# One-engine tasks per 128 tokens of a batch, emitted in the order of a list scheduler, for a gated linear attention followed by a SiLU MLP

## The chip, the core and the metric

The kernel runs on one core of a Trainium2 chip. The metric is device time in microseconds of one execution. Three runs of the kernel before gave 249.70, 249.94 and 250.22 us; their median is 249.94 us.

## The reference

Two parts follow one another. The first is a recurrent attention over 768 time steps, for 4 batches and 8 heads of dimension 48, with a state of 48x48 for each batch and head. The second is an MLP on the 3072 tokens that come out, each with 8 x 48 = 384 numbers:

```python
f = 1.0 / (1.0 + np.exp(-f_logit))
for t in range(S):
    state = f[:, :, t, :, None] * state + np.einsum('bhd,bhe->bhde', k[:, :, t], v[:, :, t])
    y[:, :, t] = np.einsum('bhd,bhde->bhe', q[:, :, t], state)
x = y.transpose(0, 2, 1, 3).reshape(B * S, H * D)      # 3072 x 384
h = x @ w_in                                           # 384 x 2048
out = (h * (1.0 / (1.0 + np.exp(-h)))) @ w_out         # 2048 x 384
```

Inputs and output are fp32. The four attention inputs have 4.7 MB each, each weight matrix 3.1 MB.

## The kernel before

Time is cut into 6 chunks of 128 steps. A **unit** below is one chunk of one batch, so 128 tokens; there are 24 units. In the kernel before, four units (the four batches of a chunk `g`) go through most steps together.

For a chunk, `load` (L85, on SyncE's queue) brings `f`, `k`, `q` and `v` as one transfer each of 768 KB. `logs` (L142, L143, ScalarE) makes log(1+exp(-f)), the negative logarithm of the gate, with one Exp and one Ln. For each unit `decay` multiplies it with a triangle of ones on TensorE (`cs`, L149, a running sum over time), takes Exp of it with both signs (`ia` L151, `a` L154, ScalarE), and scales k (`ki`, L152, GpSimd) and q (`qg`, L155, VectorE). `values` casts v (L158, GpSimd) into a padded tile `vp`, `lasts` (L164, L167) gets the decay over the whole chunk, `al`. `transposes` (L179, L181) turns q and k, `scores` (L189, L193) makes the 128x128 scores of each head and masks them, `outputs` (L209, L212) sums the state's part and the scores' part straight into the transposed `y_ps`, of which VectorE makes `xT`, the operand of the MLP. `state` (L220 to L227) brings the state on by a chunk.

The MLP works on the 512 tokens of a chunk. `mlp_in` has 16 tiles `h_ps` of three 512-column matmuls (L258) each, and a Silu on ScalarE for each (L261). `mlp_out` has 16 matmuls of 384 columns (L268) for each unit, a copy (L273) and a store on SyncE's queue (L275). The weights come by GpSimd's queue, cast to bf16 on the way (`load_w_in` L119, `load_w_out` L124).

The order of each engine's instructions is the order in which the Python code issues them. `interleave_gen` mixes generators by the cost that each yields: the MLP of chunk `g` is mixed with the attention of chunk `g + 1` and the preparation of chunk `g + 2`:

```python
first = [(mlp_in(g), MLP)]
...
    first.append((part(att, ac / 2), ac / 2))
...
second = [(mlp_out(g), MLP)]
...
    second.append((prep(g + 2, wait), prep_cost(wait)))
```

All of chunk 0's attention, the weights' issue and chunk 1's preparation are written ahead of the first `mlp_in`. ScalarE needs another function table for Exp, for Ln and for Silu as the compiled program has it; each `ACT_TABLE_LOAD` stands ahead of the instruction that needs it and carries its line.

## Time and profile before

| what | value |
|---|---|
| median of three runs | 249.94 us (249.70 to 250.22) |
| span of the profiled execution | 247.9 us; the median of the runs is 2.0 us above it |
| TensorE matmul busy | 194.1 us (78%), 1616 instructions |
| VectorE busy | 111.8 us (45%), 193 instructions |
| ScalarE busy | 126.7 us (51%), 189 instructions, 23 of them table loads |
| GpSimd busy | 56.5 us (23%), 67 instructions |
| mean granted TensorE clock | 0.986 |
| HBM traffic | 25.17 MB read, 4.72 MB written |

The span runs from the first instruction to the last; a run's time also holds what lies around it. The profiled execution's own time is not given apart from its span, so the 2.0 us between span and median stand for what lies around. Busy shares are means over stages that differ: TensorE is nearly idle in the first quarter and nearly full in the rest. A matmul's recorded length includes its way through the array, so the speed of a row of matmuls is read from the distance of their starts.

### The profile page before, as it was taken

The page shows a single profiled execution, that of the slowest core. Times are in us where ns is not written, and L with a number is a line of the kernel's source. Part 1 is how long each engine was busy: PE and PEld are TensorE (multiplying, and loading weights), DVE is VectorE, ACT ScalarE, POOL GpSimd, SP SyncE. Part 2 cuts the span into 40 slices and gives each one's busy share as a digit, 9 for nine tenths or more (in the row PEclk, how much of TensorE's full clock was granted, in tenths as well). Part 3 has the DMA queues.
Part 4 walks back from the last instruction along what each step waited for, and adds up shares of the span by engine and source line. Part 5 has one row for each costly group of instructions (what it writes and reads, how often), then busy time and mean ns, then how long its engine had stood idle before and what let it go on. Part 6 is the DMA issues. An engine that isn't in the chain of part 4 may idle for free.

```text
span 247.9 us, 3938 instructions
## 1 busy us (share of the span) xinstructions
PE 194.1 (78%) x1616; PEld 116.6 (47%) x1632; DVE 111.8 (45%) x193; ACT 126.7 (51%) x189; POOL 56.5 (23%) x67
## 2 busy tenths in 40 slices
PE   0045452008999948898999989999989999999994
PEld 0034341005546725455665546755656555663462
DVE  5064752106545434444855449563476453520011
ACT  4963147015659078766376663776543454007600
POOL 1050999046000063002700018100072000000000
PEclk9999999999999985999999999999999999999999
DMA  9999999999990104995119991189601000110011
GB/s 144 187 186 187 188 197 186 184 201 187 190 130 34 49 15 97 189 176 79 36 66 172 187 180 35 66 145 187 85 32 67 32 3 0 61 38 32 0 63 63
DMA packets 105906, 26.99 MB, mean 109 GB/s; under 512 B 99232, under 2 KB 105888, under 8 KB 105888
## 3 DMA queue, kind: packets, MB, share of 16 engines
q1 hardware_dynamic: 102208, 23.60, 61.4%
q0 software_dynamic: 3680, 3.15, 7.8%
q8 instruction: 12, 0.20, 0.4%
q14 instruction: 6, 0.05, 0.1%
HBM read 25.17 MB, written 4.72 MB: 121 GB/s over the span
## 4 chain that ended last, share of the span: by engine, by line
PE 67%; DMA 11%; SPq 10%; ACT 8%; issue 1%; DVE 1%; POOL 0%; ACTq 0%; POOLq 0%
PE h_ps L258 26%; PE o_ps L268 23%; DMA v_ld<-in_v_dram 11%; SPq L85 10%; PE y_ps L209 7%; PE t_ps L179 4%; PE a_ps L189 3%; ACT L151 2%; ACT ia L151 2%; PE cs L149 2%; ACT a L154 1%; PE d_ps L223 1%; PE d_ps L220 1%; PE al_ps L164 1%; ACT lf L143 1%
## 5 line engine op out<-in xcount | busy, mean ns | idle before, releaser
L261 ACT ACTIVATE hT<-h_ps 128x512 bf16<-128x512 f32 x96 | 57.2, 597 | 45.9 <-PE h_ps L258 43.8
L258 PE MATMUL h_ps<-xT,w_in_sb 128*128 128x512 bf16 x272 | 73.9, 388 | 2.6 <-ACT hT L261 1.2
L268 PE MATMUL o_ps<-w_out_sb,hT 128*128 128x384 bf16 x384 | 71.7, 328 | 0.0
L268 PEld LDWEIGHTS <-hT 128*128 128x128 bf16 x384 | 35.7, 98 | 26.8 <-issue 5.7
L155 DVE TENSOR_TENSOR qg<-q_ld,a 128x384 bf16<-128x384 f32 x24 | 21.7, 905 | 41.4 <-ACT a L154 41.4
L149 PE MATMUL cs<-lf,triu 128*128 128x384 bf16 x24 | 9.2, 385 | 39.8 <-ACT a L154 28.2
L258 PEld LDWEIGHTS <-w_in_sb 128*128 128x128 bf16 x288 | 26.2, 100 | 29.5 <-issue 8.0
L193 DVE TENSOR_TENSOR atm<-a_ps,triu 128x512 bf16<-128x512 f32 x48 | 30.9, 686 | 19.8 <-PE a_ps L189 19.6
L152 POOL TENSOR_TENSOR ki<-k_ld,ia 128x384 bf16<-128x384 f32 x24 | 25.3, 1054 | 50.9 <-ACT ia L151 50.9
L158 POOL CAST vp<-v_ld 128x384 bf16<-128x384 f32 x24 | 16.0, 670 | 80.0 <-DMA v_ld<-in_v_dram 63.2
L273 DVE COPY o_sb<-o_ps 128x384 f32<-128x384 f32 x24 | 13.3, 555 | 29.7 <-PE o_ps L268 29.4
L151 ACT ACTIVATE ia<-cs 128x384 f32<-128x384 f32 x24 | 11.8, 490 | 27.4 <-PE cs L149 11.4
L209 PE MATMUL y_ps<-atm,vp 128*128 128x128 bf16 x240 | 23.9, 234 | 0.2
L181 DVE COPY qk<-t_ps 128x1024 bf16<-128x1024 bf16 x24 | 16.5, 688 | 13.7 <-PE t_ps L179 13.7
L227 DVE TENSOR_TENSOR st<-d_ps,al 48x192 bf16<-48x192 f32 x40 | 14.1, 352 | 14.6 <-PE d_ps L223 14.2
L212 DVE CAST xT<-y_ps 128x384 bf16<-128x384 f32 x24 | 13.2, 552 | 12.5 <-PE y_ps L209 12.5
L209 PEld LDWEIGHTS <-vp 128*128 128x128 bf16 x240 | 17.8, 105 | 0.9 <-issue 0.9
L179 PEld LDWEIGHTS <-qg 128*128 128x128 bf16 x96 | 8.2, 108 | 19.5 <-DVE qg L155 12.0
L151 ACT ACT_TABLE_LOAD x7 | 9.0, 1283 | 15.7 <-PE cs L149 15.7
L209 PE MATMUL y_ps<-qk,st 128*128 128x128 bf16 x120 | 16.5, 219 | 0.0
L223 PEld LDWEIGHTS <-ki 128*128 128x128 bf16 x80 | 6.2, 107 | 21.6 <-issue 19.4
L179 PE MATMUL t_ps<-ident,qg 128*128 128x128 bf16 x96 | 10.7, 242 | 3.6 <-DVE qk L181 2.1
(35 smaller groups left out, 142.1 us busy)
## 6 DMA issues: line engine op xcount, KB each, us to landing
out_dram<-o_sb SPq DMA_DIRECT2D x24, 192.0 KB, 1.9
f_ld<-in_f_logit_dram SPq DMA_DIRECT2D x5, 768.0 KB, 10.8
k_ld<-in_k_dram SPq DMA_DIRECT2D x5, 768.0 KB, 6.4
q_ld<-in_q_dram SPq DMA_DIRECT2D x5, 768.0 KB, 10.8
v_ld<-in_v_dram SPq DMA_DIRECT2D x5, 768.0 KB, 11.0
w_in_sb<-in_moe_w_in_dram POOLq DMA_DIRECT2D x4, 384.0 KB, 9.5
w_out_sb<-in_moe_w_out_dram POOLq DMA_DIRECT2D x2, 768.0 KB, 17.7
f_ld<-in_f_logit_dram SPq DMA_DIRECT2D x2, 384.0 KB, 5.3
```

Of the source, the lines that this page charges most:

```text
L85: nc.sync.dma_start(out=t[:, b0:b1].rearrange("p b h d -> p (b h) d"), in_=src)
L151: nc.scalar.activation(ia, cs, AF.Exp, scale=1.0)
L152: nc.gpsimd.tensor_mul(ki[i][:, b, :, 0:D], loaded[g, "k"][:, b], ia)
L155: nc.vector.tensor_mul(qg[i][:, b, :, 0:D], loaded[g, "q"][:, b], a)
L158: nc.gpsimd.tensor_copy(v_data(g % 2, b), loaded[g, "v"][:, b])
L179: nc.tensor.transpose(t_ps[:, j, p, :], src[i][:, b, 2 * p:2 * p + 2, :], ident)
L181: nc.vector.tensor_copy(sb, t_ps)
L193: nc.vector.tensor_mul(sb[:, r], a_ps[:, r], triu[:, None, :].to_broadcast([C, NP, C]))
L209: nc.tensor.matmul(y_ps[:, t, :], l, r, start=(n == 0), stop=(n == len(terms) - 1))
L258: nc.tensor.matmul(h_ps, w_in_sb[:, kk, n * 128:(n + 1) * 128], xT[g][:, kk].rearrange("p b c -> p (b c)"), start=(kk == 0), stop=(kk == K ...
L261: nc.scalar.activation(hT[g][:, n, :], h_ps, AF.Silu)
L268: nc.tensor.matmul(o_ps, hT[g][:, n, b * C:(b + 1) * C], w_out_sb[:, n, :], start=(n == 0), stop=(n == NT - 1))
```

## The change

The kernel is rewritten. Each step of each unit becomes a **task** of one engine with a duration, a priority, the tasks it waits for and the buffer slots it takes. `schedule` plays these tasks through in Python when the kernel is built: at each moment it gives a free engine the ready task of lowest priority number; for ScalarE it stays with one kind of function (Exp and Ln together, or Silu) by a few rules of its own, and counts 1.29 for each change of kind. `planned` sorts the tasks by the start that comes out, and they are emitted in that order.

The mathematics of a unit changes in these places. The output `y` is made token-major: four 96-column matmuls with the state and eight 48-column ones with the scores (`y`), copied to bf16 (`yc`), transposed by three matmuls (`yT`) and copied into `xT` (`xc`). The decay `a` is written by ScalarE over `cs` in PSUM, and VectorE reads it there for `qg`. The chunk's last decay is four one-column matmuls into the same bank and an `al` for each unit. The state is a VectorE addition (`sd`, instead of the matmul with `ident`, L220) and two multiplications on GpSimd (`su`). The MLP works on **pairs** of units, 256 tokens: a tile `mlp` holds two tiles of the hidden layer, six 256-column matmuls (`mi`) and one Silu of 512 columns (`si`). Three PSUM banks serve `mlp`, for the MLP's input and output. Loads are one transfer for each unit and tensor for units 0 to 3, then for each pair. The weights are eight transfers issued on GpSimd after `ki` of unit 2 or 4. Stores move to GpSimd's queue, but for the last two. With `turned=24` no unit takes the branch that transposes by DMA.

```diff
-def interleave_gen(*streams):
...
+CFG = dict(
+    margin=0.35,
+    pace=4.43,
+    turned=24,
+    dma_rate=187.0,
+    w_after=(2, 2, 2, 2, 2, 2, 2, 4),
...
+    rank=dict(ld=-19.78, E=-11.45, cs=-8.27, ia=-3.88, ki=-66.76, vb=-27.12, qg=6.22, tq=-14.46, qkc=71.64,
...
+SLOTS = dict(f=6, k=6, q=6, v=6, e=2, lf=3, ia=2, qk=5, vb=6, qkT=4, atm=3, yb=3, xT=4, hT=4, sd=2, al=6, o=4,
+             st0=1, st1=1, st2=1, st3=1, mlp=3, sc=1, tq=1, cs=1, yd=1)
...
+TABLE = 1.29
+class Task:
+    def __init__(self, name, eng, dur, prio, deps=(), acq=(), use=(), mode=None, phase=None, load=0.0):
...
+        groups = [(u0,), (u0 + 1,)] if P < 2 else [(u0, u0 + 1)]
+        for us in groups:
+            for n, x in enumerate("fkqv"):
+                add((x, us), "SP", 0.35 * len(us), base(us[0]) + R['ld'] + n * 0.1, acq=[I[x, P]], load=kb(192 * len(us)))
...
+        ia = add(("ia", u), "ACT", 0.387, B + R["ia"], deps=[cs], acq=[I["ia", u]], use=[I["cs", u]], mode="exp", phase=ph)
...
+    for n in range(4):
+        add(("wi", n), "POOL", 0.8, R["wi"] + n, deps=[T["ki", cfg["w_after"][n]]], load=786.432e3 / 341e3)
...
+                if t.mode is not None and t.mode != st["mode"]:
+                    st["mode"] = t.mode
+                    begin += TABLE
...
+def planned(cfg, slots):
+
+    tasks, T = make_tasks(cfg)
+    schedule(tasks, slots, cfg, cfg["margin"])
+    return sorted(tasks, key=lambda t: (t.start, t.idx))
...
+        if kind == "E":
+            nc.scalar.activation(e, at("f", u // 2)[:, i:i + n], AF.Exp, scale=-1.0)
+        else:
+            nc.scalar.activation(at("lf", u // 2)[:, i:i + n, :, 0:D], e, AF.Ln, bias=1.0)
...
+            if kind == "si":
+                return nc.scalar.activation(at("hT", P)[:, 2 * j:2 * j + 2, :], h, AF.Silu)
+            for i in range(2):
+                n = 2 * j + i
+                for kk in range(KT):
+                    nc.tensor.matmul(h[:, i, :], w_in_sb[:, kk, n * 128:(n + 1) * 128], at("xT", P)[:, kk, :],
+                                     start=(kk == 0), stop=(kk == KT - 1))
...
+        if kind == "mo":
+            o = at("o", u)[:, 0:d_model]
+            for n in range(4 * rest[1], 4 * rest[1] + 4):
+                nc.tensor.matmul(o, at("hT", P)[:, n, i * C:(i + 1) * C], w_out_sb[:, n, :],
+                                 start=(n == 0), stop=(n == NT - 1))
...
+            (nc.sync if t.eng == "SP" else nc.gpsimd).dma_start(out=out[r0:r0 + C, :], in_=at("ob", u))
+        elif kind == "cs":
+            lf, bank = at("lf", P), at("cs", u)
+            nc.tensor.matmul(bank[:, 0:HD].rearrange("p (h d) -> p h d", d=D), triu, lf[:, i, :, 0:D],
+                             start=True, stop=True, skip_group_check=True)
+            if not last:
+                for p in range(NP):
+                    nc.tensor.matmul(bank[:, HD + p:HD + p + 1], lf[:, i, 2 * p:2 * p + 2, :], ones,
+                                     start=False, stop=True, skip_group_check=True)
+        elif kind == "ia":
+            nc.scalar.activation(at("ia", u).rearrange("p h d -> p (h d)"), at("cs", u)[:, 0:HD], AF.Exp)
+        elif kind == "a":
+            nc.scalar.activation(at("cs", u)[:, 0:HD], at("cs", u)[:, 0:HD], AF.Exp, scale=-1.0)
+        elif kind == "al":
+            nc.scalar.activation(at("al", u), at("cs", u)[:, HD:HD + NP], AF.Exp, scale=-1.0)
+        elif kind == "ki":
+            nc.gpsimd.tensor_mul(at("qk", u)[:, 1, :, 0:D], at("k", P)[:, i], at("ia", u))
+        elif kind == "vb":
+            nc.gpsimd.tensor_copy(at("vb", u), at("v", P)[:, i])
+        elif kind == "qg":
+            nc.vector.tensor_mul(at("qk", u)[:, 0, :, 0:D], at("q", P)[:, i],
+                                 at("cs", u)[:, 0:HD].rearrange("p (h d) -> p h d", d=D))
...
+        elif kind == "y":
+            y, first = at("y", u), True
+            if c:
+                for p in range(NP):
+                    nc.tensor.matmul(y[:, 2 * D * p:2 * D * (p + 1)], at("qkT", u)[:, 0, p, :], at("st", u - B)[:, p, :],
+                                     start=first, stop=False, skip_group_check=True)
+                    first = False
+            for h in range(H):
+                nc.tensor.matmul(y[:, D * h:D * (h + 1)], at("atm", u)[:, h % 2, h // 2, :], at("vb", u)[:, h, :],
+                                 start=first, stop=True, skip_group_check=True)
+                first = False
+        elif kind == "yc":
+            nc.vector.tensor_copy(at("yb", u), at("y", u))
+        elif kind == "yT":
+            t_ps = at("yT", u).rearrange("p (n c) -> p n c", c=C)
+            for n in range(KT):
+                nc.tensor.transpose(t_ps[:, n, :], at("yb", u)[:, n * 128:(n + 1) * 128], ident)
+        elif kind == "xc":
+            nc.vector.tensor_copy(at("xT", P)[:, :, i * C:(i + 1) * C],
+                                  at("yT", u)[:, 0:KT * C].rearrange("p (n c) -> p n c", c=C))
...
+        elif kind == "sd":
+            d_ps = at("d", u).rearrange("p (n w) -> p n w", w=2 * D)
+            if c:
+                nc.vector.tensor_add(at("sd", u), d_ps, at("st", u - B))
...
+        elif kind == "su":
+            for r in range(2):
+                lo = 64 * r
+                nc.gpsimd.tensor_mul(at("st", u)[lo:lo + D, :, r * D:(r + 1) * D],
...
+    with tc.manual_schedule():
+        nc.scalar.preload_act_table_set("natural_log_exp_and_others")
+        first = [t for t in tasks if t.eng == "SP"][:4]
...
+        for t in tasks:
+            if t not in first:
+                emit(t)
```

The order of the instructions shows two places on which the prediction rests. The first is **ScalarE between two groups of Silus**. Before, around the end of chunk 2's `logs` (`e`, `lf`), the 16 Silus of a chunk (`hT`), and the next `decay`:

```order
L167 ACTIVATE al<-al_ps 128x16
L142 ACTIVATE e<-f_ld 128x1536
L143 ACT_TABLE_LOAD
L143 ACTIVATE lf_112<-e 128x32x48
L261 ACT_TABLE_LOAD
L261 ACTIVATE hT<-h_ps 128x512 x16
L151 ACT_TABLE_LOAD
L151 ACTIVATE ia<-cs 128x384
L154 ACTIVATE a<-cs 128x384
```

Now, the whole stretch between the eight Silus of one pair and those of the next (L388 is `E`, L390 `L`, L438 `ia`, L440 `a`, L442 `al`, L408 `si`):

```order
L438 ACT_TABLE_LOAD
L438 ACTIVATE ia_90<-cs_142 128x384
L440 ACTIVATE cs_142<-cs_142 128x384
L442 ACTIVATE al_127<-cs_142 128x4
L388 ACTIVATE e_85<-f_61 128x768
L390 ACT_TABLE_LOAD
L390 ACTIVATE lf_87<-e_85 128x16x48
L438 ACT_TABLE_LOAD
L438 ACTIVATE ia_91<-cs_142 128x384
L440 ACTIVATE cs_142<-cs_142 128x384
L442 ACTIVATE al_128<-cs_142 128x4
L408 ACT_TABLE_LOAD
```

Before, such a turn comes once for four units; now it comes once for each pair. Up to the first Silu the program now has one load for all of the first four units' Exp and Ln; after it a load stands at each change between Exp and Ln too. There are nine such stretches after the first 16 Silus, with 6, 6, 4, 5, 4, 5, 2, 2 and 2 loads, the one back to Silu included; with one at the start and one before the first Silu they are 38, where the kernel before has 23.

The second place is **GpSimd around the weights**. Before, behind `ki` of chunk 0's units 2 and 3:

```order
L152 TENSOR_TENSOR ki_117<-k_ld,ia 128x8x48 x2
L119 DMA w_in_sb<-in_moe_w_in_dram 128x3x512 x4
L158 CAST vp_119<-v_ld 128x8x48 x2
L124 DMA w_out_sb<-in_moe_w_out_dram 128x8x384 x2
L324 MEMSET st_121 128x1536
```

Now, from `ki` of unit 2 (`qk_94`; `vb` is v's cast, `st` the state):

```order
L444 TENSOR_TENSOR qk_94<-k_68,ia_90 128x8x48
L446 CAST vb_99<-v_80 128x384
L400 DMA w_in_sb<-in_moe_w_in_dram 128x3x512 x3
L444 TENSOR_TENSOR qk_95<-k_68,ia_91 128x8x48
L505 TENSOR_TENSOR st_134<-sd_122,al_124 48x4x48 x2
L400 DMA w_in_sb<-in_moe_w_in_dram 128x3x512
L446 CAST vb_100<-v_80 128x384
L403 DMA w_out_sb<-in_moe_w_out_dram 128x4x384 x3
```

The weights are now asked for behind the values of unit 2, in smaller pieces, and no large memset follows them on GpSimd. On TensorE the first `mi` stands right behind the scores of unit 3.

## Rows read from the trace of the kernel before

**Rows 1.** The page: busy tenths and DMA rate in 40 equal slices of the span.

```profile
PE   0045452008999948898999989999989999999994
...
PEclk9999999999999985999999999999999999999999
...
GB/s 144 187 186 187 188 197 186 184 201 187 190 130 34 49 15 97 189 176 79 36 66 172 187 180 35 66 145 187 85 32 67 32 3 0 61 38 32 0 63 63
```

**Rows 2.** The page: chain of work that ended last, share of the span.

```profile
PE 67%; DMA 11%; SPq 10%; ACT 8%; issue 1%; DVE 1%; POOL 0%; ACTq 0%; POOLq 0%
```

**Rows 3.** Waits: engine, line, waited for: us in total, times, longest.

```profile
POOL vp L158 <- DMA v_ld<-in_v_dram: 63.2, 4, 21.7
...
ACT ia L151 <- PE cs L149: 11.4, 13, 2.0
```

**Rows 4.** Timeline of the first 60 us: start, us, engine, instruction.

```profile
4.75 0.52 ACT L142 ACTIVATE e<-f_ld 128x384 f32<-128x384 f32 x1 [2.74 <-DMA f_ld<-in_f_logit_dram]
...
25.44 4.16 SPq L85 DMA_DIRECT2D v_ld<-in_v_dram  x1
...
26.98 3.24 POOL L119 DMA_DIRECT2D w_in_sb<-in_moe_w_in_dram  x4
...
29.72 17.92 SPq L85 DMA_DIRECT2D f_ld<-in_f_logit_dram  x1
...
58.23 1.06 PE L258 MATMUL h_ps<-xT,w_in_sb 128*128 128x512 bf16 x2 [0.22 <-issue]
```

**Rows 5.** DMA queues from 34 to 38 us: packets, MB, share.

```profile
q0 software_dynamic: 640, 0.62, 92.2%
q1 hardware_dynamic: 643, 0.12, 27.9%
```

**Rows 6.** Groups by line and shape: busy us, mean ns of one, idle before.

```profile
L261 ACT ACTIVATE hT<-h_ps 128x512 bf16<-128x512 f32 x96 | 57.2, 597 | 45.9 <-PE h_ps L258 43.8
...
L152 POOL TENSOR_TENSOR ki<-k_ld,ia 128x384 bf16<-128x384 f32 x24 | 25.3, 1054 | 50.9 <-ACT ia L151 50.9
...
L155 DVE TENSOR_TENSOR qg<-q_ld,a 128x384 bf16<-128x384 f32 x24 | 21.7, 905 | 41.4 <-ACT a L154 41.4
...
L154 ACT ACTIVATE a<-cs 128x384 f32<-128x384 f32 x24 | 11.6, 485 | 0.0
...
L143 ACT ACT_TABLE_LOAD x8 | 10.3, 1283 | 0.1
...
L151 ACT ACT_TABLE_LOAD x7 | 9.0, 1283 | 15.7 <-PE cs L149 15.7
...
L142 ACT ACTIVATE e<-f_ld 128x768 f32<-128x768 f32 x1 | 0.8, 846 | 0.0
...
L167 ACT ACTIVATE al<-al_ps 128x16 f32<-128x16 f32 x6 | 1.1, 183 | 14.8 <-PE al_ps L164 14.8
```

**Rows 7.** Timeline, TensorE at full clock and the end.

```profile
130.17 0.39 PE L179 MATMUL t_ps<-ident,qg 128*128 128x128 bf16 x4
...
130.39 0.39 PE L179 MATMUL t_ps<-ident,ki 128*128 128x128 bf16 x4
...
136.22 0.40 PE L189 MATMUL a_ps<-qk 48*128 48x128 bf16 x8
...
136.55 1.47 PE L258 MATMUL h_ps<-xT,w_in_sb 128*128 128x512 bf16 x6
...
156.54 0.54 PE L164 MATMUL al_ps<-ones,lf 128*128 128x1 bf16 x16
...
233.72 10.56 PE L268 MATMUL o_ps<-w_out_sb,hT 128*128 128x384 bf16 x64
```

**Rows 8.** Stretches: length, PE, PEld, DVE, ACT, POOL busy, PEclk, DMA share, GB/s.

```profile
88.00:90.00 2.00, 0.32 (x1) 0.10 (x1) 1.01 (x1) 1.52 (x5) 1.34 (x2) 1.00 0.00 0
...
92.00:94.00 2.00, 1.62 (x24) 1.15 (x23) 1.06 (x3) 1.07 (x4) 2.00 (x3) 0.50 0.00 0
...
131.90:163.80 31.90, 30.57 (x281) 18.75 (x282) 18.37 (x32) 19.91 (x31) 6.82 (x8) 1.00 0.80 124
```

More of the change, by code (lines that the diff above doesn't have):

```diff
@@ L13 @@
 AF = mybir.ActivationFunctionType
[L14 removed]
 PSUM = bass.MemoryType.PSUM
[L18 to L38 removed]
+CHUNKS, BATCHES = 6, 4
@@ L55 @@
     C = 128
-    NCH = S // C
     HD = H * D
@@ L157, in values @@
-    def values(g, b):
-        nc.gpsimd.tensor_copy(v_data(g % 2, b), loaded[g, "v"][:, b])
-    def lasts(g):
-        al_ps = cps.tile([C, B, NP], F32, name="al_ps", tag="cs")
-        for b in range(B):
-            for p in range(NP):
-                nc.tensor.matmul(al_ps[:, b, p:p + 1], lf[g % 3][:, b, 2 * p:2 * p + 2, :], ones,
-                                 start=True, stop=True)
-        al = gk.tile([C, B, NP], F32, name="al")
-        nc.scalar.activation(al, al_ps, AF.Exp, scale=-1.0)
-        alast[g] = al
@@ L170 @@
[L170 to L186 removed]
+    assert (S // C, B, NT) == (CHUNKS, BATCHES, NTILES)
@@ new lines @@
+    in_psum = {"mlp", "sc", "tq", "cs", "yd"}
+    buf = {}
+    for cls, n in SLOTS.items():
+        for s in range(n):
+            shape, dt = shapes[cls]
+            buf[cls, s] = (ps if cls in in_psum else sb).tile(shape, dt, name=f"{cls}{s}")
+    triu = sb.tile([C, C], BF16, name="triu")
+    ident = sb.tile([C, C], BF16, name="ident")
+    ones = sb.tile([C, 1], BF16, name="ones")
+    w_in_sb = sb.tile([128, KT, d_ff], BF16, name="w_in_sb")
+    w_out_sb = sb.tile([128, NT, d_model], BF16, name="w_out_sb")
@@ L231, in attend @@
-    def attend(g):
-        last = g == NCH - 1
-        for s in range(B + 2):
-            if s < B:
-                transposes(g, s)
-                yield 450.0
-            if 1 <= s <= B:
-                scores(g, s - 1)
-                yield 350.0
-            if s >= 2:
-                outputs(g, s - 2)
-                yield 900.0
-                if not last:
-                    state(g, s - 2)
-                    yield 330.0
-    def attend_cost(g):
-        return B * (450.0 + 350.0 + 900.0 + (330.0 if g < NCH - 1 else 0.0))
@@ L278 @@
-    MLP = 16 * 650.0
-    def prep(g, wait):
-        yield wait
-        for b in range(B):
-            values(g, b)
-            decay(g, b)
-            yield 200.0
-        lasts(g)
-        yield 450.0
-    def prep_cost(wait):
-        return wait + B * 200.0 + 450.0
-    def part(gen, budget):
-        spent = 0.0
-        while spent < budget:
-            try:
-                c = next(gen)
-            except StopIteration:
-                return
-            spent += c
-            yield c
```

556 lines of the change are left out of this document (332 added, 224 removed).

## Prediction

> **What bounds the kernel now.** I read the slices first. TensorE's busy digits stay at 5 or below in the first nine slices of 6.2 us and at 8 or 9 in nearly all later ones, and the DMA rate is at 184 to 201 GB/s from the second slice to the eleventh [rows 1]. So there are two stages: one that waits for data, and one that TensorE fills. The chain that ended last says the same of the whole span: 67% TensorE, and 21% DMA and the DMA queue [rows 2]. The waits name the data: GpSimd waited 63.2 us for `v_ld` [rows 3]. The timeline shows why. The weights are issued at 26.98 us, and a load of the next chunk that follows on SyncE's queue, which takes 4.16 us otherwise, holds it for 17.92 us. The first MLP matmul starts at 58.23 us [rows 4]. The queues show the sharing: from 34 to 38 us the weights' queue moved 0.62 MB and the loads' 0.12 MB [rows 5]. From 58.23 us TensorE works until 233.72 + 10.56 = 244.3 us [rows 7], and 3.6 us of copy, store and landing follow to 247.9.
>
> **Speed of TensorE's rows.** From distances of starts [rows 7]: four transposes in 0.22 us (0.055 each), eight scores in 0.33 (0.041). Six 512-column matmuls in 1.47, one of them about 0.38 long, give 0.2165 each, so I take 0.108 for 256 columns. For 64 of 384 columns 10.56 less one length of 0.33 gives 0.1624. Matmuls of 48 and 96 columns are not there. They cannot be dearer than the 128-column ones (0.055), and sixteen of one column take 0.54, or 0.034 each. I take 0.030 and 0.041; the bounds move the sum by 6 us up (192 x 0.025 and 160 x 0.014, less what ScalarE hides) and 2 down.
>
> **TensorE's work.** Before: 288 x 0.2165 + 384 x 0.1624 = 124.7 us of MLP, and 50 of attention (360 products of 128 columns for `y` alone are 19.8). After: 576 x 0.108 + 384 x 0.1624 = 124.6, and 41 of attention. There the products for `y` cost 9 us, 72 transposes `yT` add 4.0, and the 16 matmuls with `ident` are gone (2.6). That is 165.6 against 175: ten less. A pair of units needs 13.9 us: 48 x 0.108 + 32 x 0.1624 + 3.5. The gain must come mostly from starting earlier. The order puts the first `mi` behind the scores of unit 3 and 5.6 us of attention.
>
> **1. To the first Silu of pair 2: 55.4 us.** A piece of 192 KB costs 4.16 / 4 = 1.04 us. The first transfer of 384 KB is there at 4.75 us [rows 4], so 2.67 us are fixed. ScalarE's order has `E` of pair 3 ahead of pair 2's Silus, so it needs the pieces of units 0 to 5 and `f` of 6 and 7: 26 x 1.04 = 27.0 us. The weights go before most of these, 3.15 MB at 187 GB/s = 16.8 us: 46.5 us. The MLP of pairs 0 and 1 (20.8 us on TensorE) starts at 23 to 25 us, when the first weights land, and lies beside this. Then ScalarE [rows 6]: `E` and `L` at 0.85 each, two loads at 1.28, two times 1.15 for `ia`, `a` and `al`, 1.0 between them because `qg` (0.9) must leave the one `cs` bank, and the load for Silu: 8.9 us.
>
> **2. Silus of pair 2: 4.7 us.** Three banks are full when ScalarE comes back. The fourth `mi` waits for the first Silu (0.6), then five at 0.65 and a last Silu.
>
> **3. Five turns of ScalarE: 81.9 us.** Here I choose. The stretches before pairs 3 to 7 have 6, 4, 5, 4 and 5 loads. With 2 or 4 long `E`/`L` and two units of 1.15 they last 13.4, 9.1, 12.1, 9.1 and 12.1 us; with 4.7 for the Silus the turns are 18.1, 13.8, 16.8, 13.8 and 16.8. TensorE needs 13.9 for a pair, so three turns are set by ScalarE and two by TensorE: 79.4. For each turn I add 0.5 for the hand-over: `ia` waited 11.4 us for `cs` in 13 cases [rows 3], 0.9 each, half of it behind a load. The planner counts one change of table where the program has up to three, so this stretch is the part that its order does not foresee. TensorE's last `mi` of pair 7 ends 0.8 before the last Silu: 141.2 us.
>
> **4. TensorE alone: 60.6 us.** Behind it stand 58.3 us of work: 192 `mi` (20.7), 160 `mo` (26.0), the rest attention. The stretches have two loads (4.9 us) here and hide. The cycle from 131.9 to 163.8 us [rows 8] holds 29.8 us of work by the same prices, so engines waiting for one another cost 7%; I take 4%, as the new order gives TensorE other work to turn to, and keep 0 to 7 for the range.
>
> **5. End and clock.** Tail 3.6. The clock fell to a granted 0.50, so 1.2 GHz, after TensorE had done 0.32 us of work in two [rows 8]; the slices show 0.8 and 0.5 [rows 1], which is (0.11 + 0.41) x 6.2 = 3.2 us of lost time or a little more. The turn before pair 3 leaves TensorE about 4 us idle. I take half of one such loss, 1.6, and in the range none to six.
>
> **Edits at no cost of their own.** On GpSimd a unit costs `ki` 1.05, the cast and the two `su` at most as much each (half the elements for a `su`), so 3.2 at most [rows 6], and a store's issue 3.24 / 4 = 0.81 [rows 4]: 95 us in 24 units, under 200. Should a store that waits stand in front of a `ki`, the next `tq` waits behind it; that is one of the rivals. VectorE was busy 111.8 us; two copies come in place of one cast and a copy or addition in place of two products. At 0.6 or less each that is 24 x 0.6 = 14 us more at most, and `qg` may fall below its 0.905 as GpSimd no longer reads beside it from the same memory, or stay [rows 6]. `a` is now written to PSUM, which no row shows: 0.4 to 0.6 where it was 0.485, so 24 x 0.12 = 3 us at most, in the range. The stores now take the weights' queue and push loads back by about 1 us each. The loads' 18.9 MB, the weights and ten stores end near 128 us, about when `E` of pair 11 wants them. The early memsets and the constants lie beside the first loads.
>
> **Sum.** 55.4 + 4.7 + 81.9 - 0.8 + 60.6 + 3.6 + 1.6 = 207.0 us of span. The median of the runs lies 2.0 above the profiled span, so **209 us**.
>
> **A rule against the rows.** Each of the eight loads ahead of `L` lasts 1.283 us, and ScalarE was idle before all of them together for 0.1 us [rows 6]: the price of a load is its own length. The Trainium skill ("ScalarE: Activation LUTs", What ACT_TABLE_LOAD costs) gives a drain of about 1.38 us on top, about 2.66 in all. By that, an estimate from the page, the 27 loads of parts 1 and 3 would add 37 us, and the sum would be 246. The rows show no such idle time, so I stay with 1.283. The same page (Table sets: the hidden batching unit) says that one set holds Exp and Ln and that such a pair needs one load. The seven loads ahead of `ia` behind an Ln [rows 6], and the order of the changed program, speak against it for everything behind the first Silu.
>
> **Rivals.**
> *The extra loads hide.* ScalarE waited 45.9 us before its Silus [rows 6], so it has idle time; if the order lets TensorE fill each stretch with `mo` and attention, TensorE sets the pace from pair 2 on: 53.5 + 134 x 1.04 + 3.6 + 2.0 = 198 us. Against it: the sums of part 3 leave no idle time in three of five turns. The same comes out if the chip's program has no loads between Exp and Ln. 0.15.
> *The clock falls in each of the six long stretches.* For: the fall in [rows 8] came from a gap around the same table changes. Six times 3.2 in place of 1.6: 227 us. Against: TensorE has `mo` to do in most of them. 0.12.
> *Every load costs twice its length*, because ScalarE empties before it: 27 x 1.283 = 35 us more, 244. The 0.1 us of idle time before eight loads [rows 6] speaks against it. 0.02. (The page's drain would be this case.)
> *TensorE never gets back to full clock (slower).* If short matmuls between waits keep it at 1.2 GHz from pair 3 to 7, a turn takes 27.8 us and not 16.4: 57 more, 266 us. It decides once some 41 us of full-speed work runs at half. Against: with the same mix the clock was back at 1.00 in the long stretch [rows 8]. 0.04.
> *The program does not do its own order*, with an in-order queue held by a store or a state update, for 10 to 15 us more: 0.05.
>
> **Numbers.** My case keeps 0.62, with 200 to 218 from the bounds: 6 up for narrow matmuls, 3 for `a`, 2 for waits; 9 down without part 3's hand-overs, the waits of part 4, the clock and 2 for narrow matmuls. 195 to 225 takes in the hidden loads and most of the late queue, and leaves the three dear rivals outside. Only the half-clock case is slower: faster 0.955, slower 0.04, and 0.005 within 0.2%, about what a measurement of this kernel can tell from no change.
>
> **What would show it.** First `mi` at 23 to 25 us and `E` of pair 3 at 46 to 47; 38 loads of 1.28 us without idle time before those inside a stretch; between 60 and 141 us `mi` waiting for `si` at the start of three turns; TensorE nearly full after 141. It is wrong if `E` of pair 3 waits for something other than its load, if TensorE is full from 55 us on, or if the granted clock is at half for more than 5 us after 60.

## The result, and the profile of the changed kernel

| | before | changed |
|---|---|---|
| median of the runs | 250.08 us (4 runs, 249.70 to 252.53) | 221.07 us (4 runs, 219.66 to 222.77) |
| ratio | | 0.8831, 95% interval 0.8774 to 0.8888 |
| profiled execution | span 247.9 us | 219.66 us, span 217.9 us |
| mean granted TensorE clock | 0.986 | 0.961 |

The change is 11.7% faster, which was forecast, and the time lies in the stated range of 195 to 225 us, but 12 us above the 209 us of the sum and above the 200 to 218 us that the prediction gives its own case. Of the 12 us 10.9 lie in the span of the profiled execution (217.9 for 207.0); the rest is that the median of the runs is 3.2 us above that span, not 2.0. The page of the changed kernel, first, by lines that answer to [rows 1, 2]: busy time of TensorE, slices (5.4 us each now), chain.

```profile
PE 184.9 (85%) x1872; PEld 137.4 (63%) x1872; DVE 102.7 (47%) x201; ACT 149.6 (69%) x230; POOL 74.9 (34%) x126
...
PE   1478899757999859969969969985999999999992
...
PEclk9999999995999979988987999999999999999999
...
GB/s 139 216 219 187 190 186 194 210 200 244 208 274 164 248 215 207 225 244 177 224 223 37 3 36 36 3 38 38 3 36 39 0 39 36 39 36 3 37 35 72
...
PE 69%; ACT 17%; DMA 4%; DVE 3%; issue 3%; SPq 1%; POOL 0%; DVEq 0%; ACTq 0%; POOLq 0%
```

The chain has changed: the data's 21% [rows 2] are down to 5%, and ScalarE has risen from 8% to 17%. The digits of TensorE dip to 5 or 6 six times from slice 9 to slice 28, where before nearly all were at 8 or 9 from the tenth slice on [rows 1]; at or behind four of the six dips the granted clock falls too. The first `mi` stands at 22.04 us (58.23 before, [rows 4]) and the last `mo` ends at 214.1 (244.3 before). So the stretch from first to last MLP matmul grew from 186 to 192 us, though TensorE is busy for less in all (184.9 us, 194.1 before): the whole gain is the start, 36 us earlier, and some 6 us of it are lost again behind.

The groups that answer to [rows 6]:

```profile
L408 ACT ACTIVATE hT<-mlp 128x512 bf16<-128x512 f32 x96 | 56.3, 597 | 32.4 <-PE mlp L412 28.9
...
L444 POOL TENSOR_TENSOR qk<-k,ia 128x384 bf16<-128x384 f32 x24 | 23.9, 995 | 58.8 <-ACT ia L438 50.5
L448 DVE TENSOR_TENSOR qk<-q,cs 128x384 bf16<-128x384 f32 x24 | 13.2, 551 | 36.9 <-ACT al L442 35.6
...
L438 ACT ACT_TABLE_LOAD x14 | 18.0, 1283 | 8.1 <-PE cs L435 7.5
...
L408 ACT ACT_TABLE_LOAD x10 | 12.8, 1283 | 0.2
```

`si` has as much work as before and waits 32.4 us for it (45.9 before). `ki` and `qg` wait 50 and 36 us for ScalarE; what stands behind them in their queues waits with them.

**Where the sum went off.** The Silus of a pair make a group on ScalarE. Their starts and ends, read from its timeline, give each part of the sum:

| part | forecast | measured | off by |
|---|---|---|---|
| 1: to the first Silu of pair 2 | 55.4 | 61.4 | +6.0 |
| 2: Silus of pair 2 | 4.7 | 4.9 | +0.2 |
| 3: five turns, pairs 3 to 7 | 81.9 | 89.4 | +7.5 |
| overlap: pair 7's last `mi` ends ahead of its last Silu | -0.8 | -0.6 | +0.2 |
| 4: TensorE from pair 7's last `mi` to the last `mo` | 60.6 | 59.1 | -1.5 |
| 5: tail | 3.6 | 3.8 | +0.2 |
| 5: clock, of its own | 1.6 | in the rows above | -1.6 |

Part 3 splits again. The five stretches without a Silu last 13.8, 9.9, 11.9, 9.9 and 11.9 us, 57.3 together, against 55.8 by the sum. The Silus last 6.2, 8.0, 6.2, 6.5 and 5.2, 32.1 together, against five times 4.7. So the price of the extra table loads was right, and what followed each stretch was not.

**Part 1, by the timeline of ScalarE** (start, us, instruction, idle time before and its releaser):

```profile
45.98 0.17 ACT L442 ACTIVATE al<-cs 128x4 f32<-128x4 f32 x1
46.05 0.84 ACT L388 ACTIVATE e<-f 128x768 f32<-128x768 f32 x1
46.91 1.28 ACT L390 ACT_TABLE_LOAD   x1
48.20 0.84 ACT L390 ACTIVATE lf<-e 128x768 bf16<-128x768 f32 x1
55.48 1.28 ACT L438 ACT_TABLE_LOAD   x1 [6.43 <-PE cs L435]
56.77 0.49 ACT L438 ACTIVATE ia<-cs 128x384 f32<-128x384 f32 x1
...
58.98 0.49 ACT L438 ACTIVATE ia<-cs 128x384 f32<-128x384 f32 x1 [1.13 <-PE cs L435]
...
61.37 4.92 ACT L408 ACTIVATE hT<-mlp 128x512 bf16<-128x512 f32 x8
```

`E` of pair 3 stands at 46.05, as forecast, but not for the forecast's reason. The prediction has it wait for `f` of units 6 and 7. That transfer, issued at 31.38 us, landed 10.9 us later (KB, us to landing):

```profile
f<-in_f_logit_dram SPq DMA_DIRECT2D x1, 384.0 KB, 10.9
```

So `f` was there at 42.3 us, when ScalarE was at the decay of unit 4, and `E` followed `al` of unit 5 without a wait: that the two times agree is chance. Everything behind `E` costs what was taken, but for 6.43 us in which ScalarE waits for `cs` of unit 6. TensorE has it late in its order:

```profile
44.58 0.32 PE L431 MATMUL cs<-lf,triu 128*128 128x384 bf16 x1 [1.77 <-DVE qk L448]
...
48.62 0.61 PE L465 MATMUL sc<-qkT 48*128 48x128 bf16 x8 [0.25 <-DVE qkT L456]
50.36 1.44 PE L422 MATMUL mlp<-w_out_sb,hT 128*128 128x384 bf16 x4 [1.13 <-DMA w_out_sb<-in_moe_w_out_dram]
...
51.91 1.49 PE L422 MATMUL mlp<-w_out_sb,hT 128*128 128x384 bf16 x4
...
53.51 1.48 PE L422 MATMUL mlp<-w_out_sb,hT 128*128 128x384 bf16 x4
54.79 0.53 PE L431 MATMUL cs<-lf,triu 128*128 128x384 bf16 x1
```

Ahead of it are the attention of units 4 and 5, which waits for ScalarE step by step, and twelve `mo` that need the last piece of `w_out`. That piece is late because its issue stands on GpSimd behind `ki` of unit 4, which waits 13.81 us for `ia`:

```profile
43.48 0.99 POOL L444 TENSOR_TENSOR qk<-k,ia 128x384 bf16<-128x384 f32 x1 [13.81 <-ACT ia L438]
44.42 0.81 POOL L403 DMA_DIRECT2D w_out_sb<-in_moe_w_out_dram  x1
```

And those `mo` run at half speed: four of them take 1.2 to 1.3 us from their start to that of the next instruction, not 0.65. The stretches (length, PE, PEld, DVE, ACT, POOL busy, PEclk, DMA share, GB/s) show TensorE half idle and then the granted clock at 0.50, so 1.2 GHz:

```profile
46.00:48.00 2.00, 1.22 (x21) 0.94 (x21) 1.99 (x5) 1.98 (x3) 1.55 (x3) 1.00 1.27 183
48.00:50.00 2.00, 0.96 (x15) 0.69 (x16) 1.76 (x4) 1.03 (x2) 0.00 (x0) 0.60 1.26 209
50.00:52.00 2.00, 1.64 (x8) 0.96 (x8) 0.73 (x2) 0.00 (x0) 0.00 (x0) 0.50 1.19 238
52.00:54.00 2.00, 2.00 (x12) 1.11 (x10) 0.96 (x3) 0.00 (x0) 0.62 (x1) 0.50 1.19 245
```

**Part 3, by the turn before pair 4.** ScalarE, then VectorE, then TensorE:

```profile
93.80 0.17 ACT L442 ACTIVATE al<-cs 128x4 f32<-128x4 f32 x1
93.99 1.28 ACT L408 ACT_TABLE_LOAD   x1
96.18 0.60 ACT L408 ACTIVATE hT<-mlp 128x512 bf16<-128x512 f32 x1 [0.91 <-PE mlp L412]
...
101.01 3.22 ACT L408 ACTIVATE hT<-mlp 128x512 bf16<-128x512 f32 x5 [1.85 <-PE mlp L412]
```

```profile
94.00 0.55 DVE L448 TENSOR_TENSOR qk<-q,cs 128x384 bf16<-128x384 f32 x1 [2.65 <-ACT al L442]
94.47 0.35 DVE L488 COPY xT<-tq 128x384 bf16<-128x384 bf16 x1
```

```profile
91.35 1.47 PE L422 MATMUL mlp<-w_out_sb,hT 128*128 128x384 bf16 x8
94.88 0.61 PE L454 MATMUL tq<-ident,qk 128*128 128x128 bf16 x8 [2.06 <-DVE xT L488]
95.32 3.21 PE L412 MATMUL mlp<-xT,w_in_sb 128*128 128x256 bf16 x18
```

The copy `xc` of the next pair, whose transposes ended at 91.5 us, stands in VectorE's order behind a `qg` that starts, by its row, when the last `al` of the stretch has ended. `tq` has one bank and waits for `xc`; TensorE, in order too, idles 2.06 us. So when ScalarE comes back, the `mlp` banks are not filled yet, and the matmuls that fill them run at half speed for the most part: 18 `mi` take 3.14 us to the next start, 0.17 each, against the sum's 0.108. The granted clock there is 0.55 and 0.60 (96 to 98 and 98 to 100 us).

The same wait of 2.06 us stands ahead of `tq` in the turns of pairs 5 and 6. In that of pair 5 the clock fell too (0.50 from 114 to 116 us); in that of pair 6 it stayed at 1.00 from 128 to 134 us:

```profile
130.84 0.61 PE L454 MATMUL tq<-ident,qk 128*128 128x128 bf16 x8 [2.06 <-DVE xT L488]
131.28 2.13 PE L412 MATMUL mlp<-xT,w_in_sb 128*128 128x256 bf16 x18
```

So a gap of this length does not decide by itself whether the clock falls.

### The profile page after: what moved, and what is told of

Read it like the earlier page. It is cut to its first block, busy times and chain, and to the rows that moved or that the text cites. A ratio compares the mean times of both kernels' runs of the same rounds, so it can differ in the third digit from the quotient of the medians.

```text
span 217.9 us, 4591 instructions
## 1 busy us (share of the span) xinstructions
PE 184.9 (85%) x1872; PEld 137.4 (63%) x1872; DVE 102.7 (47%) x201; ACT 149.6 (69%) x230; POOL 74.9 (34%) x126
## 4 chain that ended last, share of the span: by engine, by line
PE 69%; ACT 17%; DMA 4%; DVE 3%; issue 3%; SPq 1%; POOL 0%; DVEq 0%; ACTq 0%; POOLq 0%
PE mlp L412 30%; PE mlp L422 21%; PE tq L454 5%; ACT L438 4%; PE sc L465 3%; ACT lf L390 3%; DMA w_out_sb<-in_moe_w_out_dram 3%; PE yd L478 2%; PE cs L431 2%; ACT L390 2%; ACT L388 2%; ACT ia L438 2%; ACT e L388 2%; DMA f<-in_f_logit_dram 2%; PE yd L474 2%
## 5 line engine op out<-in xcount | busy, mean ns | idle before, releaser
L408 ACT ACTIVATE hT<-mlp 128x512 bf16<-128x512 f32 x96 | 56.3, 597 | 32.4 <-PE mlp L412 28.9
L412 PE MATMUL mlp<-xT,w_in_sb 128*128 128x256 bf16 x576 | 72.2, 284 | 3.3 <-DVE o L425 1.7
L422 PE MATMUL mlp<-w_out_sb,hT 128*128 128x384 bf16 x384 | 71.9, 332 | 1.1 <-DMA w_out_sb<-in_moe_w_out_dram 1.1
L412 PEld LDWEIGHTS <-w_in_sb 128*128 128x128 bf16 x576 | 57.6, 102 | 12.9 <-issue 3.3
L469 DVE TENSOR_TENSOR atm<-sc,triu 128x512 bf16<-128x512 f32 x48 | 30.9, 685 | 34.1 <-PE sc L465 34.1
L444 POOL TENSOR_TENSOR qk<-k,ia 128x384 bf16<-128x384 f32 x24 | 23.9, 995 | 58.8 <-ACT ia L438 50.5
L505 POOL TENSOR_TENSOR st<-sd,al 48x192 bf16<-48x192 f32 x40 | 20.0, 501 | 22.3 <-DVE sd L499 14.7
L454 PE MATMUL tq<-ident,qk 128*128 128x128 bf16 x192 | 17.1, 241 | 8.8 <-DVE xT L488 6.2
L438 ACT ACT_TABLE_LOAD x14 | 18.0, 1283 | 8.1 <-PE cs L435 7.5
L438 ACT ACTIVATE ia<-cs 128x384 f32<-128x384 f32 x24 | 11.7, 489 | 13.9 <-PE cs L435 9.8
L454 PEld LDWEIGHTS <-qk 128*128 128x128 bf16 x192 | 13.4, 108 | 11.3 <-issue 7.1
L456 DVE COPY qkT<-tq 128x1024 bf16<-128x1024 bf16 x24 | 16.5, 688 | 8.5 <-PE tq L454 8.5
L425 DVE COPY o<-mlp 128x384 f32<-128x384 f32 x24 | 13.3, 553 | 14.0 <-PE mlp L422 13.9
L446 POOL CAST vb<-v 128x384 bf16<-128x384 f32 x24 | 11.7, 503 | 9.8 <-issue 5.0
L408 ACT ACT_TABLE_LOAD x10 | 12.8, 1283 | 0.2
```

The source lines that it names most:

```text
L408: return nc.scalar.activation(at("hT", P)[:, 2 * j:2 * j + 2, :], h, AF.Silu)
L412: nc.tensor.matmul(h[:, i, :], w_in_sb[:, kk, n * 128:(n + 1) * 128], at("xT", P)[:, kk, :], start=(kk == 0), stop=(kk == KT - 1))
L422: nc.tensor.matmul(o, at("hT", P)[:, n, i * C:(i + 1) * C], w_out_sb[:, n, :], start=(n == 0), stop=(n == NT - 1))
L425: nc.vector.tensor_copy(at("ob", u), at("o", u)[:, 0:d_model])
L438: nc.scalar.activation(at("ia", u).rearrange("p h d -> p (h d)"), at("cs", u)[:, 0:HD], AF.Exp)
L444: nc.gpsimd.tensor_mul(at("qk", u)[:, 1, :, 0:D], at("k", P)[:, i], at("ia", u))
```

## The experiments

The theory after this reading: the loads cost what they last; the rest of the miss is two pieces of work behind a late one in an in-order queue (`wo` 3 on GpSimd, `xc` on VectorE), and the clock that falls in the gaps. Ratios are to the kernel before on the same chip.

**e1: one table set.** Asks again for the set that holds Exp and Ln at each switch back from Silu; 20 loads, not 38.

```diff
+        mode = "exp"
         for t in tasks:
+            if t.mode == "exp" and mode == "silu":
+                nc.scalar.preload_act_table_set("natural_log_exp_and_others")
+            mode = t.mode or mode
             if t not in first:
                 emit(t)
```

> The changed kernel, with one request for the table set that holds Exp and Ln ahead of each stretch that follows Silus: 20 table loads instead of 38, nothing else moved. Theory (the 18 extra loads are the late work of the middle part: 18 x 1.283 = 23 us on ScalarE, which come out at TensorE through late Silus, through VectorE's product for q standing in front of the copy of y, and through the scaled k standing in front of the last weight piece): turns of pairs 3 to 7 of 13.5 to 14.5 us instead of 15.2 to 20, Silus of pair 2 from 54 to 58 us instead of 61.4, median 199 to 206 us. Rival (the loads hide beside other work and the order itself makes TensorE wait): 215 us or more.

200.22 us (199.54 to 201.18), ratio 0.7988 [0.7936, 0.804]; mean clock 0.990. The turns of pairs 3 to 7 are 14.4, 14.1, 14.2, 14.1 and 13.7 us, TensorE's pace. The first Silu of pair 2 comes at 60.4, hardly earlier: with fewer loads ScalarE waits 7.42 us for `cs` of unit 6, not 6.43. 18 loads of 1.283 are 23.1 us; 20.9 came back. So the loads did not hide: their cost, with the gaps and the low clock that came with them, was nine tenths of their length. As TensorE now sets the turns, this is no measure of what a single load costs.

**e2: the last piece of `w_out` issued with the others.**

```diff
+    wo3 = next(t for t in tasks if t.name == ("wo", 3))
+    tasks.remove(wo3)
+    tasks.insert(next(i for i, t in enumerate(tasks) if t.name == ("wo", 2)) + 1, wo3)
```

> The changed kernel with the fourth piece of w_out issued on GpSimd right behind the third, no longer behind the scaled k of unit 4. Theory (TensorE's wait at 42 to 50 us and the fall of the clock behind it come from this piece, issued at 44.4 and landing at 50.3 us): the mo row goes on at 42 us, the running sum of unit 6 moves from 54.8 to about 49, the Silus of pair 2 start at 55 to 57 us instead of 61.4, median 214 to 217 us. Rival (the piece is not what is waited for; the loads of pair 3 or unit 5's chain hold the same place): start of the Silus within 1.5 us of 61.4 and a median of 219 to 222.

214.91 us (213.84 to 216.20), 0.8573 [0.8513, 0.8634]; clock 0.984. The time is the theory's, the place is not: the first Silu of pair 2 moves by 0.9 us only, to 60.5, with 4.64 us of ScalarE's wait for `cs` left and the clock still at 0.50 around 50 us. What became shorter is the turns: 18.6, 16.4, 16.6, 16.4, 17.0 in place of 20.0, 17.9, 18.0, 16.4, 17.0. Their stretches without a Silu are the same (57.3 us in both), and so are TensorE's three waits of 2.06 us for `xc`, but the granted clock is 1.00 in every window of 2 us from 54 to 130 us. The turn of pair 4:

```profile
92.55 0.61 PE L457 MATMUL tq<-ident,qk 128*128 128x128 bf16 x8 [2.06 <-DVE xT L491]
93.00 2.13 PE L415 MATMUL mlp<-xT,w_in_sb 128*128 128x256 bf16 x18
```

So 4.4 us of part 3's miss are the clock in the turns of pairs 3 to 5. The move that was made for part 1 shifted TensorE's work in time; why the clock then stayed up is not shown.

**e3: `xc` ahead of the waiting `qg`,** where nothing between needs that `qg` (five places).

```diff
+    for xc in [t for t in tasks if t.name[0] == "xc"]:
+        dve = [t for t in tasks if t.eng == "DVE"]
+        qg = dve[dve.index(xc) - 1]
+        if qg.name[0] == "qg":
+            p, n = tasks.index(qg), tasks.index(xc)
+            if not any(qg in t.deps or t.name[0] == "cs" for t in tasks[p + 1:n]):
+                tasks.insert(n, tasks.pop(p))
```

> The changed kernel with five of VectorE's products for q (qg of the pair's second unit) moved behind the copy xc that stood right after them. Theory (TensorE's idle 2 us ahead of tq in a turn come from xc standing behind a qg that waits for ScalarE's late a, and the clock falls there): in the turns of pairs 4 to 7 the wait of tq for xc is gone, the granted clock stays at 1.00 there, the turns lose 2 to 4 us each, median 207 to 214 us. Rival (ScalarE's stretch itself sets the turn, and TensorE merely waits a step later, at the fourth mi): turns shorter by under 1 us, median 217 to 221.

216.08 us (212.05 to 216.65), with a mean clock of 0.984 in the lowest run and 0.968 to 0.976 in the others; the spread is too wide for a ratio. In the profiled one, 216.57 us, the wait of `tq` for `xc` is gone, and the turns of pairs 4, 5 and 6 shrink by 3.1, 1.4 and 1.6 us, while pair 2 comes 3.2 us later, behind a longer stretch of low clock.

**e13: e2 and e3 together, all 38 loads kept.**

> The changed kernel with all its 38 table loads, but with the fourth piece of w_out moved forward and VectorE's five products for q moved behind xc, the two moves of earlier runs together. Theory (the blind sum priced ScalarE's turns rightly and missed two things that stand in line behind ScalarE on GpSimd and VectorE; without these it holds): Silus of pair 2 at 55 to 61 us, turns of pairs 4 and 6 near 14.5 and 15, those of 3, 5 and 7 at 16.5 to 18.6, median 206 to 212 us. Rival (with the two waits gone TensorE waits elsewhere behind ScalarE and the clock falls there): 213 us or more.

213.07 us (211.85 to 213.87), 0.8468 [0.8423, 0.8513]; clock 0.992. By the median that is the rival's time, if by 0.07 us. But the rival's mechanism is not there: the granted clock is 1.00 in every window of 2 us from 56 to 130 us, and TensorE no longer waits for `xc`. The turns are 18.6, 14.8, 16.6, 14.8, 17.0, which is 81.8 us where part 3 had 81.9, and 3.1 us less than in e2. The rows at 94 us show the first three Silus start without a wait:

```profile
93.46 1.28 ACT L418 ACT_TABLE_LOAD   x1
94.75 1.57 ACT L418 ACTIVATE hT<-mlp 128x512 bf16<-128x512 f32 x3
97.37 3.22 ACT L418 ACTIVATE hT<-mlp 128x512 bf16<-128x512 f32 x5 [1.04 <-PE mlp L422]
```

Part 1 stays: `56.07 ACT_TABLE_LOAD` follows 4.31 us of waiting for `cs`, and pair 2 starts at 62.3 us. This wait is in every variant that keeps the order otherwise (3.98 us in e5), and no run took it away.

**e5: e1 and e2 together.**

> Both the one table set and the early fourth piece of w_out. Theory (two causes that partly overlap, as without the extra loads the scaled k of unit 4 is 2.6 us earlier already): 1 to 4 us less than with the one table set alone, 196 to 204 us. Rival (with the loads gone nothing waits for the piece): the same as with the one table set alone, within 1 us.

196.48 us (195.66 to 197.00), 0.7833 [0.7784, 0.7882]; the fastest version found, ahead of both kernels. Stretches of the changed kernel, then of e5:

```profile
70.00:80.00 10.00, 6.22 (x70) 4.50 (x69) 3.60 (x8) 9.32 (x13) 4.04 (x6) 0.96 1.18 226
...
90.00:100.00 10.00, 7.94 (x74) 5.58 (x73) 4.01 (x9) 6.97 (x10) 4.07 (x7) 0.83 1.05 224
```

```profile
70.00:80.00 10.00, 10.00 (x119) 7.70 (x117) 6.24 (x12) 9.59 (x15) 3.85 (x7) 1.00 1.10 218
...
90.00:100.00 10.00, 10.00 (x114) 7.34 (x113) 6.48 (x13) 9.51 (x16) 5.05 (x8) 1.00 1.20 228
```

TensorE is busy without a gap at full clock, from 50 to 180 us. The move of `w_out` is worth 3.7 us here, against e1: the first Silu of pair 2 comes at 56.8 us for 60.4, as ScalarE's wait for `cs` is 3.98 us for 7.42. `xc` was left where it was, and its wait no longer shows.

**e6: what the clock alone costs.** In the turns of pairs 4 to 6, ten useless 384-column matmuls into an idle `mlp` bank where TensorE waits ahead of `tq`. They overwrite nothing that is read.

```diff
+            if t in late:
...
+                for _ in range(10):
+                    nc.tensor.matmul(idle[:, 0:384], ident, w_out_sb[:, 0, :], start=True, stop=True, skip_group_check=True)
```

> The changed kernel with ten matmuls of 384 columns of no use (identity times a piece of w_out, into the bank that the next mi overwrites; 1.6 us at full clock) ahead of tq in the turns of pairs 4, 5 and 6, where TensorE waits about 2 us for the copy xc; all waits stay. Theory (part of what the extra loads cost is the fall of the granted clock behind such a wait): clock at 1.00 from 92 to 100 and from 110 to 118 us, the Silus of pairs 4 and 5 take 5 to 7 us instead of 8.1 and 6.2, median 216 to 219 us. Rival (ScalarE's lateness alone sets the turns and the clock costs nothing): 220.5 us or more, with 5 us of useless work in it.

218.07 us (216.84 to 219.34), 0.8702 [0.8651, 0.8753]; turns of pairs 4 and 5 16.4 and 16.6 in place of 17.9 and 18.0. The same place in TensorE's timeline:

```profile
93.54 1.79 PE L535 MATMUL mlp<-w_out_sb,ident 128*128 128x384 bf16 x10
95.76 0.61 PE L454 MATMUL tq<-ident,qk 128*128 128x128 bf16 x8 [0.43 <-DVE xT L488]
96.20 2.13 PE L412 MATMUL mlp<-xT,w_in_sb 128*128 128x256 bf16 x18
```

The wait for `xc` is still there, filled with work of no use; the 18 `mi` behind it take 2.13 us and not 3.21. The Silus of pair 4 last 6.5 us, not 8.0. So in two turns the fall of the clock, not the wait itself, cost 1.4 to 1.5 us each, as between the changed kernel and e2. In the turn of pair 6, where the clock had not fallen, the filling changed nothing (16.4 both). That the filling kept the clock up is not shown: e2 has the same gaps unfilled, and the clock stayed up there as well.

**Four runs on the kernel before** ask which part of the rewrite buys the early start.

*e7*: the first MLP ahead of chunk 1's preparation.

```diff
         lasts(0)
+        for _ in mlp_in(0):
+            pass
         logs(1, 0, B)
...
-            first = [(mlp_in(g), MLP)]
+            first = [(mlp_in(g), MLP)] if g else []
```

> The kernel before with the MLP of chunk 0 issued ahead of chunk 1's logs and preparation (mlp_in alone, mlp_out beside the preparation), nothing of the rewrite. Theory (the whole gain of the change is the earlier start of the MLP, since its stretch from the first MLP matmul to the last is 6 us longer than before): the first MLP matmul at 34 to 40 us instead of 58, chunk 1's at 72 to 80 instead of 95, median 228 to 238 us. Rival (an early MLP only leaves chunk 1's attention without cover, and units, pairs and token-major y are needed for the gain): 243 us or more.

251.66 us, ratio 1.0006 [0.996, 1.0051]. The first MLP matmul moves from 58 to 35.0 us, yet chunk 1's `mlp_in` starts in earnest at 100 us as it did, and the time is the rival's: the loads of chunk 2 now stand behind stores on SyncE's queue, and the DMA rate falls to 1 to 99 GB/s in slices 9 to 11.

*e10*: as e7, and chunk 2's loads issued right behind the first `mlp_in`.

```diff
+        for _ in mlp_in(0):
+            pass
+        for name in "fkqv":
+            load(2, name)
         logs(1, 0, B)
...
-        load(2, "f")
...
```

> The kernel before with the early MLP of chunk 0 of the run before, and with chunk 2's four loads issued ahead of mlp_out instead of behind its stores on SyncE's queue. Theory (the early start was given back because the loads of chunk 2 stood behind the first stores: the DMA rate fell to 21 GB/s at 60 to 70 us and chunk 1's mlp_in came at 100 us as before): no idle DMA between 50 and 70 us, chunk 1's mlp_in at 74 to 84 us, median 229 to 239 us. Rival (in the old structure an early MLP is worth nothing, as chunk 1's attention is then without cover): mlp_in of chunk 1 later than 90 us and 245 us or more.

249.83 us, 0.9932 [0.9893, 0.9971]. The loads are no longer late, and still little is won: chunk 1's attention now runs with no MLP beside it, at a low clock.

```profile
70.00:80.00 10.00, 8.03 (x86) 6.58 (x86) 7.67 (x14) 1.43 (x1) 0.35 (x1) 0.56 1.06 173
80.00:90.00 10.00, 4.33 (x55) 2.96 (x53) 6.96 (x13) 3.90 (x7) 3.40 (x4) 0.78 1.26 185
```

So an early MLP alone is worth nearly nothing in the order of the kernel before. That the mixing by pairs, which leaves MLP work beside the attention of the next units, is what keeps the early start is argued from these rows; no run changed the pairs alone.

*e8*: one table set, as in e1, for the kernel before; 10 loads, not 23.

```diff
+    def exp_set():
+        if table[0] != "exp":
+            nc.scalar.preload_act_table_set("natural_log_exp_and_others")
+            table[0] = "exp"
...
+            table[0] = "silu"
             nc.scalar.activation(hT[g][:, n, :], h_ps, AF.Silu)
```

> The kernel before with one request for the set that holds Exp and Ln at the start and behind each group of Silus: 10 table loads instead of 23, nothing moved. Theory (before, the loads bind only where ScalarE's stretch holds back TensorE, at 87 to 98 us and little in the turns of 32 us; those ahead of 58 us lie beside loads): 6 to 9 us less, 241 to 244 us. Rival (they cost as much for each load as in the changed kernel, 21 us for 18): 235 us or less.

244.81 us, 0.9761 [0.9708, 0.9815]: 5.8 us for 13 loads, 16.7 us of ScalarE. A third of their length was on the path, where in the changed kernel it was nine tenths.

*e9*: the loads of the kernel before, cut into one transfer per unit.

```diff
-        nc.sync.dma_start(out=t[:, b0:b1].rearrange("p b h d -> p (b h) d"), in_=src)
+        for b in range(b0, b1):
+            nc.sync.dma_start(out=t[:, b], in_=src[:, (b - b0) * H:(b - b0 + 1) * H])
```

> The kernel before with each load of f, k, q and v cut into one transfer of 192 KB for each batch. Theory (the loads' rate of 187 GB/s before and 216 to 219 in the changed kernel's first 14 us hangs on the size of the transfers): over 205 GB/s in the slices from 6 to 25 us, the values of chunk 1 4 to 6 us earlier, median 243 to 247 us. Rival (the rate comes from something else, as where the data go): 184 to 190 GB/s as before, and 249 to 251 us.

247.14 us, 0.9876 [0.9809, 0.9944]; the DMA rate stays at 169 to 193 GB/s in the second to sixth slices. Smaller transfers are not why the changed kernel reads at 216 to 219 in its second and third slices. What gained 3 us was not told apart.

**Two runs let the planner make a new order,** with one table set: *e11* has all weights behind unit 2, *e12* has `w_in` behind unit 1 and all of `w_out` behind unit 2.

```diff
-    w_after=(2, 2, 2, 2, 2, 2, 2, 4),
+    w_after=(2, 2, 2, 2, 2, 2, 2, 2),
...
+                nc.scalar.preload_act_table_set("natural_log_exp_and_others")
...
```

> The changed kernel with one table set behind each group of Silus (20 loads), and the planner told to issue the last piece of w_out behind unit 2 like the others; the planner makes its whole order anew. Theory (with the tables as the planner counts them, its order holds on the chip, and the piece costs nothing any more): 194 to 199 us, like the version in which the piece alone was moved (196.5). Rival (a new order is worse by chance): over 200 us.

215.69 us (215.33 to 216.81), 0.8588 [0.8512, 0.8665], 19 us above e5, which has the same pieces at nearly the same place. VectorE's `o` waits 38.1 us for `mo` (13.9 in the changed kernel), once 14.5 us on end, and TensorE has gaps again:

```profile
DVE o L425 <- PE mlp L422: 38.1, 11, 14.5
```

```profile
50.00:60.00 10.00, 6.70 (x67) 5.18 (x68) 5.74 (x12) 3.52 (x6) 4.12 (x8) 0.69 1.10 229
```

```diff
-    w_after=(2, 2, 2, 2, 2, 2, 2, 4),
+    w_after=(1, 1, 1, 1, 2, 2, 2, 2),
```

> As the run before, with w_in's four pieces issued behind unit 1 (w_out's behind unit 2); the order is made anew. Theory (what is left is the start: TensorE waits for the first weights until 22 us): the first MLP matmul at 18 to 20 us, median 191 to 196 us. Rival (the weights only take the loads' place, so the units behind come later by as much): 196 to 201 us.

212.77 us (211.93 to 213.57), 0.8458 [0.8394, 0.8522]. The first Silu comes at 20.4 us, the 3 to 4 us earlier that were expected, but TensorE is then busy 6.68 and 7.99 us of ten from 30 to 50 us. Both theories failed: a changed input gives another order, and its waits are not the old ones. Why these orders are so much worse (whether, as seems likely, the planner's ranks fit only the input that they were found with) was not tried.

## Why the prediction was right in direction and 12 us short

- **What bounds the kernel** was read rightly. The gain is the earlier start: first `mi` at 22.04 (forecast 23 to 25). e7 and e10 add what the prediction did not see, that in the old order an early first MLP alone brings nothing.
- **Speed of TensorE's rows.** Full-clock rows confirm it: eight 48-column matmuls take 0.21 us to the next start, 0.026 each (0.030 taken), four of 96 columns 0.17, 0.0425 each (0.041 taken; the kernel before has the same, from 155.72 to 155.89 us). Part 4 came out at 59.1 for 60.6, with the 4% for mutual waits a little too much.
- **Part 1 failed, by 6.0 us.** The step is "so it needs the pieces of units 0 to 5 and `f` of 6 and 7 ... Then ScalarE", which let `E` wait for data and ScalarE run through from `E` to the load for Silu. `E` came at 46.05 by chance: its data had landed 3.8 us before, and it followed `al` at once. Behind `L` ScalarE waited 6.43 us for `cs` of unit 6. The order of TensorE, which could be read before, has that `cs` behind the attention of units 4 and 5 and twelve `mo`. Of this wait the late weight piece explains 1 to 2 us (e2: 4.64 left, the first Silu 0.9 earlier), and 3.4 us where the extra loads are gone (7.42 in e1, 3.98 in e5). How much each of the rest takes, the chain through units 4 and 5 or the low clock, stays open.
- **Part 3 failed, by 7.5 us, in its last step,** "for each turn I add 0.5 for the hand-over", and in the clock. The stretches by loads and Exp work were 57.3 us against 55.8; the Silus took 32.1 against 23.5. The hand-over was sized by a wait of `ia`, but the wait that counted was TensorE's for `xc`, which stood behind a `qg` on VectorE: 3.1 us, from e2 to e13. The other 4.4 us, from the changed kernel to e2, are the clock in the turns of pairs 3 to 5, with the same stretches and the same waits. With both gone, in e13, the turns are 81.8 us for 81.9, closer in sum than one by one.
- **The clock's 1.6 us** were too few: 4.4 us in part 3, and a share of part 1 that is not known. The prediction thought of one fall; the slices show one at 49 to 54 us and lower digits in five more, up to 120 us. It counts none to six falls as possible, but its bounds of 200 to 218 us have no term upward for them.
- **The signs.** Of the three named for a wrong prediction, the one on the clock came true: by the windows of 2 us it was at half for some 10 us after 60, in three stretches of about 3.4 us. The one on `E` of pair 3 came true in its sense, as ScalarE's own order held it and not its load. Of the signs named for a right one, `mi` waiting for `si` at the start of three turns did not come: `mi` waited 1.6 us for `si` in all, while `tq` waited 6.2 us for `xc` and `cs` 5.3 us for `qg`.
- **The range** held, but not by its own working. The bounds 6, 3 and 2 upward add up to 220 us, not 218, and 221.07 lies above both; the narrow matmuls and `a`, for which 9 us of them were kept, cost next to nothing beyond what was taken. It is the width kept for other cases, up to 225, that covered the two waits and the clock.
- **Two small slips** changed little. The terms named for part 2 add up to 4.45 us, not 4.7 (4.92 measured). Of the seven loads ahead of `ia` [rows 6] only four stand behind an Ln; the other three stand behind a Silu.
- **The price of a load** was right: 1283 ns, and ScalarE was idle for 0.2 us in all before the ten loads ahead of Silus, with the next instruction 0.01 to 0.02 us behind. The drain that the Trainium skill gives ("ScalarE: Activation LUTs", What ACT_TABLE_LOAD costs) does not show here either. The same page's rule that Exp and Ln share one set (Table sets: the hidden batching unit) holds only if the set is asked for: this program loaded 38 times, and 20 times when it was.
- **VectorE** was forecast to have up to 14 us more and went down from 111.8 to 102.7: `qg` with its operand in PSUM takes 551 ns against 905 [rows 6], the gain that was named as possible; `yc` takes 555 and `xc` 354 ns. `a` written to PSUM takes 486 ns, for 485 before.
- **GpSimd** was costed by its sum (95 us at most, 74.9 measured). Its order was the point: 50.5 us of waiting in `ki`, with a weight's issue behind one.
- **Rivals.** *The extra loads hide* (198) did not happen, but its price for a program without loads between Exp and Ln is close: e1 200.22. *The clock falls in each stretch* came true in part, for 4.4 us in part 3 and not the 18 us that it puts on the forecast. *An in-order queue held*, put at 10 to 15 us and a chance of 0.05, is the nearest to what happened: moving the two held pieces gave back 8.0 us (221.07 to 213.07; 3.6% by the ratios), of which 4.4 us are the clock that no longer fell in the turns. It deserved more, because the order of the queues was there to be read.
